# q and k turned on VectorE in blocks, scores on 32-row groups: a change to a fused attention and channel-mix kernel

## The chip, the core and the metric

One NeuronCore of a Trainium2 chip runs the whole program. Five engines work side by side, each through its own fixed sequence of instructions: TensorE (PE; its weight loads are listed apart as PEld), VectorE (DVE), ScalarE (ACT), GpSimd (POOL, here mostly an issuer of DMAs) and SyncE (SP, another issuer). They wait for one another through semaphores. The metric is the device time of one execution in microseconds, as the median of several runs; lower is better.

## What is computed

Sliding-window attention with linear distance biases for 8 batches, 8 heads, 576 positions and 64 dimensions a head, and a channel mix with two gates over its output. Shortened:

```python
scores = scale * q @ k.T                       # per batch and head, 576 x 576
mask = (rel >= 0) & (rel < 128)                # rel = query position - key position
scores = where(mask, scores - slope[h] * abs(rel), -1e9)
attn = softmax(scores);  x = attn @ v          # heads side by side: 576 x 512 a batch
xk = mu_k * x + (1 - mu_k) * x_prev            # x_prev: one position earlier
xr = mu_r * x + (1 - mu_r) * x_prev
out = sigmoid(xr @ w_r) * (relu(xk @ w_k) ** 2 @ w_v)
```

## The kernel before

**Staging.** All matmuls take bf16. A matmul contracts over the partitions, so the scores need q and k with the 64 dimensions of a head on the partitions, while in memory a position's 64 dimensions lie side by side. q and k are therefore loaded with positions on the partitions and turned. Heads go in four pairs, g = 0 to 3, two heads of 64 rows each filling 128 partitions. Positions are cut into four chunks of 128 (SM = 512) and a tail of 64.

**How q and k are turned**, by batch:

- Batch 0 comes first and has its own path in two parts (staging tiles in qx_buf, L1097, L1100 and qk_quad with two runs).
- Batches 1 and 2 (WIDE): wide_load, L463, brings runs of four positions, four heads at a time. qk_quad (L1053) turns each 64x64 block by a matmul against an identity, 32 a head pair; ScalarE or VectorE copies the result from PSUM to qk_buf (L663, a helper that makes every copy).
- Batches 3 to 5: full_load, L498, makes eight loads of 1,024 short runs a batch into cb_buf. qk_some with halves (L804) turns 32 blocks for two head pairs at once; ScalarE copies.
- Batches 6 and 7 (XB): the same loads, but the DMA engines turn them (flip, L502, eight DMA transposes a batch on SP's queue, into qx_buf).
- The tail of 64 positions of each batch is loaded apart into ts_buf (L482, L488), and turned into tt_buf by four matmuls (tails_full, L879; batches 1 to 3) or by one DMA transpose (L595; batches 4 to 7).

**Scores and attention.** For a head pair, `scores` (L693) makes twelve matmuls on 64 rows: six pieces (256, 256, 256, 128, 64, 64 query columns for five key chunks) for each of the two heads, whose row groups 0 to 63 and 64 to 127 work side by side. They fill both two-bank PSUM tiles (duo, class p2). ScalarE makes exp of each half (L707, 128x1024), VectorE multiplies with the exponentials of the bias (L720). `attend` multiplies with v (L749, 18 matmuls), VectorE divides by the row sums (L755, L760) into xu, `out_t` turns xu back (L787; by DMA in batches 6 and 7, L869), and `shift` makes xk and xr (L847, L854 twice).

**Channel mix.** `channel_mix` handles up to 512 positions at once: the matmuls with w_k (L958), relu on ScalarE (L965), the square on VectorE (L931) or ScalarE (L929), the matmuls with w_r (L976) and its tanh (L983), the matmuls with w_v (L992), and the product on VectorE (L997), then the store on SP's queue (L1022). SQ says which engines may square: both in the first three passes, VectorE alone after that.

**Order.** No engine's order is written by hand. Each piece of work becomes a node with engines that may do it, an assumed length, its dependencies, the buffers it takes and frees, and a rank. `Plan.run` plays them through once when the program is built, and emits the instructions in the order found; the chip keeps that order on each engine, so that an instruction which must wait holds all behind it on its engine. `rank` sorts attention by batch and head pair, moved by the tables LEAD and SHIFT per engine, against the channel mix. `paced` holds the turns of a batch back until enough channel mix is planned. `pe_key` lets work on 64 rows follow other work on 64 rows, as TensorE must change its row mode between them. Loads stand in POOL's queue in the order of LOADS, then batch by batch: a (q and k), b (tails), c (v).

Of the kernel before, what the change touches and what calls it, by code (L numbers as in the profile page):

```python
# [9 lines left out]
FP32 = mybir.dt.float32  # L10
# [23 lines left out]
class Plan:  # L34
# [148 lines left out]
def kernel(  # L183
# [30 lines left out]
    NQ, NA, NX, NV, NC = 4, 4, 3, 2, 2  # L214
    XB = range(6, B)
    XO = range(6, B)
    X0 = 16
# [6 lines left out]
    WIDE = (1, 2)  # L224
    PART_WIDE = True
    QK1 = (ACT, DVE)
    TW = (0,)
    QUAD = 0.040
    RUN = {2: 64 * 284 / 345.0, NF: 128 * 284 / 390.0}
# [5 lines left out]
    WAIT = 7.42  # L235
    COST = {'first': 1.28, 'v': 1.15, 'q': 0.944, 'ts': 0.66, 'tv': 0.58, 'w': 0.88, 'run4': 1.0, 'run2': 1.03, 'flip': 1.0, 'mu': 1.0, 'x': 1.0}
    SS = ()
    OH = ()
    QM = 2
    OM = 0  # L240
# [4 lines left out]
    def SQ(order):  # L245
        return (DVE, ACT) if order < 3 else (DVE,)
# [7 lines left out]
    XTT = range(4, B)  # L254
    MMASK = False
    VDEP = 1
    TCOST = 1.5
    KLAST = 1
# [13 lines left out]
    ts_buf = many(2, [128, H, D], BF16, "ts")  # L272
    tt_buf = many(2, [128, G, 3, 64], BF16, "tt")
    qk_buf = many(NQ, [128, 2, SM], BF16, "qk")
    qx_buf = many(2, [128, 2, G, SM], BF16, "qx")
    half_buf = qx_buf[0].rearrange("p i g s -> p (i g s)").rearrange(
        "p (a i r h d) -> p a i r h d", a=2, i=2, r=2, d=D)
    part_buf = qx_buf[0].rearrange("p i g s -> p (i g s)")[:, 2048:4096].rearrange(
        "p (i h r d) -> p i h r d", i=2, r=2, d=D)
    wide_buf = [c.rearrange("p i r h d -> p (i r h d)").rearrange(  # L280
        "p (i h r d) -> p i h r d", i=2, r=NF, d=D) for c in cb_buf]
    stage = qx_buf[1].rearrange("p i g s -> p (i g s)").bitcast(FP32).rearrange(
# [36 lines left out]
    plan = Plan(dict(qx=2, p2=2, p1=N1, pt=4 - N1, qk=NQ, at=NA, xu=NX, vs=NV, cb=NC, ts=2, tt=2, xt=2, dl=2, dl0=4,  # L319
# [10 lines left out]
    def dve_t(n, fast=1):  # L330
# [4 lines left out]
        PE: (19.41, 21.75, 20.3, 20.77, 27.74, 12.48, 14.5, 17.35, 11.67, 21.63),  # L335
        ACT: (-36.25, -14.3, 13.52, -0.46, 8.81, -1.54, 38.45, -38.45, -6.19, 11.9),
        DVE: (-3.5, -13.64, -11.95, 8.63, -28.73, 12.81, 21.66, -2.46, -14.09, 3.03),
# [3 lines left out]
        PE: {(0, 0): 33.45, (1, 0): 0.96, (2, 0): 26.3, (3, 0): 24.3, ('fkk',): -39.43, ('p1', 'fkk'): 4.02, ('p1', 'fxk'): 5.15},  # L341
        ACT: {(1, 0): -17.87, (2, 0): 20.9, (3, 0): 41.7, ('frl',): 48.19, ('rl', 'fp1'): 40.97, ('rs', 'fp1'): -20.02},
        DVE: {(0, 0): -69.5, (1, 0): 89.05, (1, 1): -21.81, (1, 2): -35.86, (2, 0): -19.05, (3, 0): -5.03, ('fp1', 'frs'): -11.82, ('frl',): -102.36, ('ot', 'fp1', 'frs'): 6.45},
# [98 lines left out]

    def blanks(after):
# [8 lines left out]
        for t in range(2):  # L452
            late(tt_buf[t][:, :, 2], 0.0, 0.17)
# [22 lines left out]
    def tail_load(b):  # L476
        h = Hold("ts")
        g = virtual("ts", [h])
        ns = []
        if b in TW:  # L480
            for i in range(2):
                ns.append(dma(POOL, 104, issue_t(128), lambda e, i=i: nc.gpsimd.dma_start(  # L482
                    out=ts_buf[h.idx].rearrange("p h d -> p (h d)")[:, 256 * i:256 * i + 256],
                    in_=(q, k)[i][b, :, SM:S].rearrange("h (c r) d -> h c (r d)", r=4)), [g], kind="ts"))
            return h, ns
        for i in range(2):
            src = (q, k)[i][b, :, SM:S].rearrange("h p d -> p h d")
            ns.append(dma(POOL, 128 * TCOST, issue_t(512), lambda e, i=i, src=src: nc.gpsimd.dma_start(  # L488
                out=ts_buf[h.idx][64 * i:64 * i + 64], in_=src), [g], kind="ts"))
        return h, ns  # L490

    def wide_load(b, h, g, h0, h1):
        return [run_load(lambda: wide_buf[h.idx], i, b, 0, NF, h0, h1, [g]) for i in range(2)]

    def full_load(b, i, h, g):
        src = (q, k)[i][b, :, 0:SM].rearrange(
            "h (r p) d -> p h r d" if b in XB else "h (p r) d -> p h r d", p=128)
        return [dma(POOL, 256, issue_t(1024), lambda e, r=r: nc.gpsimd.dma_start(  # L498
            out=cb_buf[h.idx][:, i, r], in_=src[:, :, r]), [g], kind="q") for r in range(NF)]

    def flip(b, i, j, g):
        return dma(SPE, FLIP * RATE, FISSUE, lambda e: nc.sync.dma_start_transpose(  # L502
            out=qx_buf[xbh[b].idx][:, i, :, 128 * j:128 * j + 128],
            in_=cb_buf[ch[b].idx][:, i, j].rearrange("p h d -> p (h d)")),
            [g, (cl[b][NF * i + j], FWAIT)], (), [ch[b]], FLAT, True)
# [54 lines left out]
    def load_step(what):  # L560
# [14 lines left out]
        elif what == "t":  # L575
            th[0], tl[0] = tail_load(0)
# [12 lines left out]
    cw, ch, cl, xbh, xbl, tth, ttl, ttg = {}, {}, {}, {}, {}, {}, {}, {}  # L589

    def tail_flip(b):
        htt, hs = Hold("tt"), th[b]
        g = plan.add(VIR, 0.0001, 0.0001, [], (0,), None, [htt])
        tth[b], ttg[b] = htt, g
        ttl[b] = [dma(SPE, FLIP * RATE, FISSUE, lambda e: nc.sync.dma_start_transpose(  # L595
            out=tt_buf[htt.idx][:, :, 0:2].rearrange("p g t c -> p g (t c)"),
            in_=ts_buf[hs.idx].rearrange("p h d -> p (h d)")),
            [g] + [(x, FWAIT) for x in tl[b]], (), [hs], FLAT, True)]

    def batch_load(b, what):  # L600
        if what == "a":
            ch[b] = Hold("cb")
            g_ = virtual("cb", [ch[b]])
            if b not in WIDE:
                cl[b] = full_load(b, 0, ch[b], g_) + full_load(b, 1, ch[b], g_)
            else:
                cw[b] = [wide_load(b, ch[b], g_, 4 * j, 4 * j + 4) for j in range(2)]
        elif what == "b":
            th[b], tl[b] = tail_load(b)
            if b in XB:  # L610
                xbh[b] = Hold("qx")
                g_ = virtual("qx", [xbh[b]])
                xbl[b] = [flip(b, i, j, g_) for i in range(2) for j in range(NF)]
            if b in XTT:
                tail_flip(b)
# [49 lines left out]
    def scores(b, g, parts, bias, hq, ha, deps, prio, need, free):  # L665
# [9 lines left out]
        def emit(e):  # L675
            qk = qk_buf[hq.idx] if hq.cls == "qk" else qx_buf[hq.idx][:, :, g]
# [119 lines left out]
    def halves(n, block):  # L796

        hp = [Hold("p1"), Hold("p1")]

        def emit(e):  # L800
            for i in range(n):
                src, c = block(i)
                for r in range(2):
                    nc.tensor.transpose(  # L804
                        one(hp[r]).bitcast(BF16)[:, c:c + 64], src[64 * r:64 * r + 64],
                        ident[64 * r:64 * r + 64, 64 * r:64 * r + 64])

        return hp, emit
# [492 lines left out]
```

## Time and profile before

| What | Value |
|---|---|
| median of three runs (lowest, highest) | 235.77 us (235.13, 236.39) |
| span of the profiled execution | 233.9 us |
| granted TensorE clock in it | full (1.000) |
| DMA, share of the POOL-issued queue's packets in 16 engines' span | 97.6%, 96,016 packets |
| loads of q and k into cb, issue to landing (median) | 6.8 to 7.5 us for 128 KB, 10.0 to 10.3 us for 256 KB |
| turns by DMA into qx (16) | 7.8 us each, issue to landing |

The span runs from the first to the last instruction of one execution. The profile names an instruction by its source line and the tiles that it writes and reads, without buffer numbers. Busy time of TensorE is a union of overlapping matmuls, whose single lengths (some 190 ns for a small one) include the array's latency; what a block costs the engine is read from the chain of waits or from the distance between starts. Durations on DVE and ACT stand as they are. ScalarE's copies to qk take 616 ns on average (37 of 128x512), its exp of 128x1024 takes 1,039 ns (56 of them), VectorE's mask product 684 ns (56), its quotient xu 819 ns (28).

### The profile page before, as it was taken

The page shows a single profiled execution, that of the slowest core. Times are in us where ns is not written, and L with a number is a line of the kernel's source. Part 1 is how long each engine was busy: PE and PEld are TensorE (multiplying, and loading weights), DVE is VectorE, ACT ScalarE, POOL GpSimd, SP SyncE. Part 2 cuts the span into 40 slices and gives each one's busy share as a digit, 9 for nine tenths or more (in the row PEclk, how much of TensorE's full clock was granted, in tenths as well). Part 3 has the DMA queues.
Part 4 walks back from the last instruction along what each step waited for, and adds up shares of the span by engine and source line. Part 5 has one row for each costly group of instructions (what it writes and reads, how often), then busy time and mean ns, then how long its engine had stood idle before and what let it go on. Part 6 is the DMA issues. An engine that isn't in the chain of part 4 may idle for free.

```text
span 233.9 us, 6461 instructions
## 1 busy us (share of the span) xinstructions
PE 225.3 (96%) x2586; PEld 138.3 (59%) x2615; DVE 189.6 (81%) x424; ACT 164.7 (70%) x294; POOL 93.5 (40%) x120
## 2 busy tenths in 40 slices
PE   8999799999999999999999999979999999999994
PEld 7676666665756755555855765535564744445462
DVE  7497998999998999887999999879899965324252
ACT  3769998979986969979997585845674626236261
POOL 8796655679972980794195740000000000000000
PEclk9999999999999999999999999999999999999999
DMA  7999999999999999899999999952314121121212
GB/s 172 184 163 193 187 170 201 193 172 192 157 143 126 145 143 179 70 163 175 127 189 108 180 158 206 169 93 92 118 32 121 69 76 45 46 90 48 90 45 90
DMA packets 121565, 31.09 MB, mean 133 GB/s; under 512 B 108216, under 2 KB 117696, under 8 KB 121536
## 3 DMA queue, kind: packets, MB, share of 16 engines
q0 software_dynamic: 96016, 16.26, 97.6%
q1 hardware_dynamic: 23776, 13.84, 27.0%
q10 hardware_dynamic: 1744, 0.59, 1.1%
q8 instruction: 20, 0.33, 0.6%
q14 instruction: 9, 0.07, 0.1%
HBM read 33.56 MB, written 9.44 MB: 184 GB/s over the span
## 4 chain that ended last, share of the span: by engine, by line
PE 75%; DMA 13%; DVE 4%; ACT 3%; issue 2%; POOL 1%; POOLq 0%; DVEq 0%; ACTq 0%
PE uno L992 25%; PE uno L958 21%; PE uno L976 12%; PE duo L749 6%; PE duo L693 5%; DMA ts<-in_k_dram 4%; DMA xt<-xu 3%; DMA wk_sb<-in_moe_w_k_dram 3%; DMA vs<-in_v_dram 3%; PE uno L787 3%; ACT at L707 2%; PE uno L1053 1%; PE uno L804 1%; DVE kk L931 1%; POOL vs L467 1%
## 5 line engine op out<-in xcount | busy, mean ns | idle before, releaser
L992 PE MATMUL uno<-wv_sb,kk 128*128 128x512 bf16 (+2 forms) x277 | 70.8, 373 | 1.5 <-DVE kk L931 0.5
L707 ACT ACTIVATE at<-duo 128x1024 bf16<-128x1024 f32 (+2 forms) x68 | 63.9, 986 | 8.5 <-PE duo L693 8.5
L958 PE MATMUL uno<-xk,wk_sb 128*128 128x256 bf16 (+2 forms) x412 | 69.1, 313 | 0.6
L965 ACT ACTIVATE rl<-uno 128x256 bf16<-128x256 f32 (+2 forms) x104 | 46.8, 481 | 13.3 <-PE uno L958 11.5
L958 PEld LDWEIGHTS <-wk_sb 128*128 128x128 bf16 x416 | 38.5, 98 | 20.2 <-issue 0.2
L983 ACT ACTIVATE rs<-uno 128x512 bf16<-128x512 f32 x36 | 21.7, 606 | 34.5 <-PE uno L976 32.5
L992 PEld LDWEIGHTS <-kk 128*128 128x128 bf16 x296 | 26.8, 98 | 28.3 <-DVE kk L931 1.3
L997 DVE SCALAR_TENSOR_TENSOR ot<-rs,uno 128x512 f32<-128x512 bf16 (+2 forms) x37 | 24.8, 669 | 19.7 <-PE uno L992 16.3
L467 POOL DMA_DIRECT2D vs<-in_v_dram x32 | 28.4, 903 | 28.7 <-PE duo L749 21.3
L720 DVE TENSOR_TENSOR at<-at,mask 128x1024 bf16<-128x1024 bf16 x56 | 37.3, 684 | 2.2 <-ACT at L707 2.0
L976 PE MATMUL uno<-wr_sb,xr 128*128 128x512 bf16 x138 | 36.7, 379 | 0.9 <-DVE ot L997 0.5
L931 DVE TENSOR_TENSOR kk<-rl 128x256 bf16<-128x256 bf16 (+2 forms) x96 | 31.3, 340 | 7.6 <-ACT rl L965 6.2
L854 DVE SCALAR_TENSOR_TENSOR xr<-dl,mu_sb,xt 128x576 bf16<-128x576 bf16 (+1 forms) x32 | 24.9, 779 | 0.3
L854 DVE SCALAR_TENSOR_TENSOR xk<-dl,mu_sb,xt 128x576 bf16<-128x576 bf16 (+1 forms) x32 | 24.6, 778 | 0.0
L749 PEld LDWEIGHTS <-at 128*128 128x128 bf16 x576 | 21.5, 98 | 5.1 <-issue 0.6
L663 ACT COPY qk<-uno 128x512 bf16<-128x512 bf16 (+1 forms) x40 | 21.3, 598 | 3.4 <-PE uno L1053 1.7
L760 DVE TENSOR_TENSOR xu<-duo,rc 128x640 bf16<-128x640 f32 x28 | 22.7, 819 | 0.2
L976 PEld LDWEIGHTS <-xr 128*128 128x128 bf16 x144 | 13.5, 98 | 15.9 <-issue 0.7
L498 POOL DMA_DIRECT2D cb<-in_k_dram x20 | 17.7, 922 | 5.0 <-DMA vs<-in_v_dram 3.2
L749 PE MATMUL duo<-vs,at 128*128 128x65 bf16 x448 | 19.1, 194 | 0.1
L498 POOL DMA_DIRECT2D cb<-in_q_dram x20 | 17.8, 924 | 1.7 <-DMA cb<-in_k_dram 0.7
L663 ACT COPY xt<-uno 128x576 bf16<-128x576 bf16 (+2 forms) x28 | 15.9, 578 | 2.4 <-PE uno L787 2.3
(81 smaller groups left out, 209.1 us busy)
## 6 DMA issues: line engine op xcount, KB each, us to landing
out_dram<-ot SPq DMA_DIRECT2D x30, 256.0 KB, 5.5
vs<-in_v_dram POOLq DMA_DIRECT2D x32, 128.0 KB, 7.6
cb<-in_q_dram POOLq DMA_DIRECT2D x20, 128.0 KB, 6.8
cb<-in_k_dram POOLq DMA_DIRECT2D x20, 128.0 KB, 7.5
out_dram<-ot SPq DMA_DIRECT2D x10, 128.0 KB, 1.7
wk_sb<-in_moe_w_k_dram POOLq DMA_DIRECT2D x2, 512.0 KB, 7.6
cb<-in_q_dram POOLq DMA_DIRECT2D x4, 256.0 KB, 10.0
cb<-in_k_dram POOLq DMA_DIRECT2D x4, 256.0 KB, 10.3
```

The costliest lines, as they stand in the source:

```text
L467: return dma(POOL, 256, issue_t(1024), lambda e: nc.gpsimd.dma_start(out=vs_buf[h.idx][:, j, :, 0:D], in_=v[b, :, 128 * j:128 * j + 128].r ...
L498: return [dma(POOL, 256, issue_t(1024), lambda e, r=r: nc.gpsimd.dma_start(out=cb_buf[h.idx][:, i, r], in_=src[:, :, r]), [g], kind="q") f ...
L663: (nc.scalar.copy if e == ACT else nc.vector.tensor_copy)(out=out, in_=in_)
L707: lambda e, ah=ah, w=w, hp=hp: nc.scalar.activation(out=ah(), in_=two(hp)[:, :, 0:w], func=AF.Exp, scale=float(scale)), (), [hp])
L720: nc.vector.tensor_tensor(out=a, in0=a, in1=m, op=ALU.mult)
L749: nc.tensor.matmul(a[:, hl, t - t0], lhsT=at[:, lo:lo + 128], rhs=vs[:, u, 2 * g + hl, :] if u < NF else tvb[:, 2 * g + hl], start=(u == u ...
L854: lambda e: nc.vector.scalar_tensor_tensor(out=buf[hk.idx][:, g, e0 + c0:e0 + c1], in0=dls(), scalar=mu[:, g:g + 1], in1=xc(1), op0=ALU.mu ...
L931: nc.vector.tensor_tensor(out=out, in0=in_, in1=in_, op=ALU.mult)
L958: nc.tensor.matmul(one(hp)[:, 0:n], lhsT=wk_sb[:, po, 128 * fo:128 * fo + 128], rhs=xk_buf[hx.idx][:, po, c0:c1], start=(po == 0), stop=(p ...
L965: a = op(ACT, act_t(n), [s], pr, lambda e, hp=hp, hr=hr: nc.scalar.activation(out=rl_buf[hr.idx][:, 0:n], in_=one(hp)[:, 0:n], func=AF.Rel ...
L976: nc.tensor.matmul(one(hp), lhsT=xr_buf[hx.idx][:, po, 128 * c:128 * c + 128], rhs=wr_sb[:, po], start=(po == 0), stop=(po == NPO - 1))
L992: nc.tensor.matmul(one(hv)[:, a:b], lhsT=kk_buf[hk.idx][:, fo, o:o + 128], rhs=wv_sb[:, fo, a:b], start=(fo == 0), stop=(fo == NFO - 1))
```

## The change

In batches 1 to 7 there is one path for q and k. `quad_load` loads four heads over 128 partitions: partition 32h + p holds 18 consecutive positions of head h, 4,608 adjacent bytes in memory, 1,152 bf16 in SBUF, the tail of 64 positions included. There are four such loads a batch (q and k, two quartets). `turn` reads such a row as 576 words of four bytes, that is two neighbouring dimensions, and transposes its eighteen 32x32 blocks in one VectorE instruction. Afterwards partition 32h + w holds the dimensions 2w and 2w+1 of every position, position by position, in qt_buf: dimensions of even and of odd number lie at every second bf16. `scores4` then makes the scores of four heads at once on the row groups 0, 32, 64 and 96: two accumulating matmuls a piece, one over the even and one over the odd dimensions, in two halves that each fill both duo tiles. Key chunk 4 has 64 positions; the other 64 columns are set to zero once (n_pad).

What falls away: wide_load, full_load, flip, tails_full, tail_flip, qk_some and qk_full, the copies to qk and the separate tail loads of batches 1 to 7. The first three steps of batch 0 keep their path; their bf16 copies now lie in the second raw buffer. Squares of every pass may run on either engine. The planner's tables (LEAD, SHIFT, COST, WAIT) have other numbers, and pe_key groups 32-row work too.

```diff
-        if rows == 64 and n.rows[0] == 64:
+        if rows != 128 and n.rows[0] == rows:
             return (-1e8,) + tuple(key)
...
     def SQ(order):
-        return (DVE, ACT) if order < 3 else (DVE,)
+        return (DVE, ACT)
...
-    cb_buf = many(NC, [128, 2, NF, H, D], BF16, "cb")
+    raw_buf = many(NC, [128, 2, 2, TB * D], BF16, "raw")
+    qt_buf = many(NT, [128, S + KW, 2], BF16, "qt")
...
+    def quad_load(b, i, c, h, g):
+        src = (q, k)[i][b, 4 * c:4 * c + 4].rearrange("h (p r) d -> (h p) (r d)", r=TB)
+        return dma(POOL, QUADKB, issue_t(128), lambda e: nc.gpsimd.dma_start(
+            out=raw_buf[h.idx][:, i, c], in_=src), [g], kind="quad")
...
-            if b not in WIDE:
-                cl[b] = full_load(b, 0, ch[b], g_) + full_load(b, 1, ch[b], g_)
-            else:
-                cw[b] = [wide_load(b, ch[b], g_, 4 * j, 4 * j + 4) for j in range(2)]
-        elif what == "b":
-            th[b], tl[b] = tail_load(b)
...
+            cl[b] = [[quad_load(b, i, c, ch[b], g_) for i in range(2)] for c in range(2)]
...
+    def turn(b, c):
+
+        hq, n, res = Hold("qt"), None, []
+        for i in (1, 0):
+            def emit(e, i=i):
+                nc.vector.transpose(
+                    out=qt_buf[hq.idx][:, S * i:S * i + S].rearrange("p s t -> p (s t)").bitcast(FP32)
+                    .rearrange("p (q t) -> p t q", t=TB),
+                    in_=raw_buf[ch[b].idx][:, i, c].bitcast(FP32).rearrange(
+                        "p (t w) -> p t w", w=32))
...
+    def scores4(b, c, half, hq, has, deps):
+
+        pieces, m0 = (QUAD0, QUAD1)[half]
...
+            for (u, q0, n) in pieces:
+                c0 = BASE[u] + q0 - 128 * u - a0
+                for t in range(2):
+                    for j in range(4):
+                        r = 32 * j
+                        nc.tensor.matmul(
+                            two(hps[j // 2])[:, j % 2, c0:c0 + n],
+                            lhsT=qt[r:r + 32, S + 128 * u:S + 128 * u + 128, t],
+                            rhs=qt[r:r + 32, q0:q0 + n, t],
+                            start=(t == 0), stop=(t == 1), skip_group_check=True)
...
+        for c in range(2):
+            hq, y = turn(b, c)
+            has = [Hold("at"), Hold("at")]
+            s0, m0 = scores4(b, c, 0, hq, has, y)
+            s1, m1 = scores4(b, c, 1, hq, has, y + [(s0, 0.0)])
+            for j in range(2):
+                g = 2 * c + j
+                prio = (0, b, 0, g)
+                r, hx = attend(b, g, 0, NJ, has[j], [m0[j], m1[j]] + vl[b], prio)
```

The pieces are QUAD0 = (chunk 0, 256 columns; chunk 1, 256) and QUAD1 = (chunk 2, 256; chunk 3, 192; chunk 4, 64). There are two raw buffers (NC = 2, a batch each) and three qt buffers (NT = 3, a quartet each).

More of the change, by code (lines that the diff above doesn't have):

```diff
@@ L223 @@
     RATE = 284.0
[L224 to L227, printed above, removed]
     QUAD = 0.040
-    RUN = {2: 64 * 284 / 345.0, NF: 128 * 284 / 390.0}
+    RUN = {2: 64 * 284 / 345.0}
+    QUADKB = 576 * 284 / 390.0
     FLIP = 1.0
@@ L451, in blanks @@
             late(tv_buf[t][0:64, :, D], 1.0)
-        for t in range(2):
-            late(tt_buf[t][:, :, 2], 0.0, 0.17)
+        late(tt_buf[0][:, :, 2], 0.0, 0.17)
+        n_pad.extend(dve_op(0.1, lambda e, t=t: nc.vector.memset(qt_buf[t][:, 2 * S:S + KW], 0.0),
+                            [after], (0, 31)) for t in range(NT))
         for t in range(NA):
@@ L587, in load_step @@
             batch_load(1, what)
[L589 to L598, printed above, removed]
+    ch, cl = {}, {}
     def batch_load(b, what):
@@ L894, in tails @@
         hs = th[b]
-        if b in XTT:
-            plan.follow(last["tt"], ttg[b])
-            last["tt"] = ttg[b]
-            return tth[b], ttl[b]
-        if b not in TW:
-            return tails_full(b, prio, htt, hs)
         hp = Hold("p1")
@@ L922 @@
     of = out.rearrange("b s m -> (b s) m")
-    n_hw = 39 + sum(4 if g in FT else 2 for g in range(3)) + 8 * len(XB) + len(XTT) + G * len(XO)
+    n_hw = 39 + sum(4 if g in FT else 2 for g in range(3)) + G * len(XO)
     n_split = -n_hw % 8
@@ L1060, in qk_quad @@
         w = 64 * nr
-        ys = [op(QK0 if b == 0 else QK1, {ACT: act_t(2 * w), DVE: dve_t(2 * w)}, [t], prio + (3,),
+        ys = [op(QK0, {ACT: act_t(2 * w), DVE: dve_t(2 * w)}, [t], prio + (3,),
                  lambda e, r=r: copy_any(
```

256 lines of the change are left out of this document (66 added, 190 removed).

## The prediction

> **What bounds the kernel now.** I read the busy shares first, then the chain of waits, then the stages.
>
> ```profile
> span 233.9 us, 6461 instructions
> PE 225.3 (96%) x2586; PEld 138.3 (59%) x2615; DVE 189.6 (81%) x424; ACT 164.7 (70%) x294; POOL 93.5 (40%) x120
> ...
> PE   8999799999999999999999999979999999999994
> ...
> DVE  7497998999998999887999999879899965324252
> ACT  3769998979986969979997585845674626236261
> ```
>
> TensorE is busy nearly everywhere, VectorE is full for two thirds of the span and half idle after that. A busy TensorE is not proof, so the chain of waits decides: 75% of it is TensorE, and its largest other share, 13% DMA, lies mostly in the first 28 us. From about 30 us on, TensorE's own instructions follow one another, and what it executes is what the span costs:
>
> ```profile
> 42.38 0.49 PE uno L1053 x32
> ...
> 43.42 0.55 PE duo L693 x12
> 43.97 0.38 PE uno L1053 x32
> ...
> 60.80 0.57 PE uno L804 x32
> ...
> 62.12 0.22 PE uno L879 x4
> ...
> 65.09 0.56 PE uno L787 x10
> 65.64 0.55 PE duo L693 x12
> ```
>
> Columns: start, length, line, count. L1053, L804 and L879 are the turns of q and k by identity matmuls; L693 is one head pair's scores. All stand on the path. The stages (busy us of each engine in a stretch):
>
> ```profile
> 24.00:36.00 12.00, 10.70 (x238) 8.07 (x237) 11.35 (x28) 11.77 (x28) 7.14 (x10) 1.00 1.86 180
> 36.00:140.00 104.00, 102.74 (x1366) 65.31 (x1383) 98.39 (x197) 89.43 (x157) 68.20 (x82) 1.00 1.90 156
> 140.00:200.00 60.00, 58.29 (x463) 31.66 (x471) 50.78 (x103) 34.90 (x56) 0.00 (x0) 1.00 0.55 100
> 200.00:234.00 34.00, 30.70 (x171) 16.58 (x172) 11.55 (x26) 12.38 (x25) 0.00 (x0) 1.00 0.20 70
> ```
>
> The order is PE, PEld, DVE, ACT, POOL. The change takes work from TensorE, where it pays at once, and puts some on VectorE, which from 36 to 140 us has 5.6 us free of 104. That is the question of this case.
>
> **The sum.** Terms are against the profiled execution, 233.9 us; the median of the runs, 235.77 us, lies 1.9 us above it.
>
> *Turns taken off TensorE.* Batches 3 to 5: 192 matmuls of L804 in 6 blocks of 0.57 us, 3.4 us. Batches 1 and 2: 256 of L1053 in 8 blocks of 0.38 to 0.52 us, 3.4 us. Tails: three blocks of L879 at 0.22 us, 0.7 us. Batches 6 and 7 have none: their q and k are turned by DMA. **-7.5 us.**
>
> *Scores on 32-row groups.* Today a pair of heads costs 0.55 us, so four heads cost 1.10 us. The chain's eight L992 matmuls of 512 columns in 1.73 us give 0.42 ns a column. A pair streams 256+256+256+128+64+64 = 1024 columns in each of two row groups at once: 0.43 us, so 0.12 us of each block is fill and switching. New: 256+256+256+192+64 columns, twice because each matmul holds half of the 64 dimensions: 2048 columns, 0.86 us for four heads if all four groups stream at once, plus two fills of 0.12, 1.10 us: no change, **0**. No row shows four groups, nor operands read at every second element. Lower end: fills hidden, 14 x -0.24 = -3.4 us. Upper end: groups go two at a time or the step of two halves the stream, 14 x 0.86 = +12 us. I take 0, since two groups start 4 ns apart in the present score blocks and 32 loads and 32 matmuls of L804 pass in 0.57 us (18 ns a pair), so that four pairs (72 ns) fit under 256 columns (108 ns).
> The Trainium skill, in "TensorE: Matmul & The Clock Gate", section "Measured speedup vs the span model", gives four row groups 3.07 times one at 512 columns, not 4. By that as an estimate 0.86 becomes 1.12 us, and the sum would end 14 x 0.26 = 3.6 us higher. No run here shows it yet.
>
> *Turns put on VectorE.* 28 instructions (7 batches, two quartets, q and k) of 576 four-byte words a partition. The nearest row is one element a cycle over the same count:
>
> ```profile
> L854 DVE SCALAR_TENSOR_TENSOR xr<-dl,mu_sb,xt 128x576 bf16<-128x576 bf16 x28 | 22.7, 812 | 0.3
> L447 DVE MEMSET at<- 128x64 bf16 x4 | 0.3, 112 | 0.0
> L429 DVE MEMSET vs<- 128x32 bf16 x2 | 0.2, 85 | 0.1
> ```
>
> 0.81 us each, 22.7 us in all. They write words 72 bytes apart. The vs memset writes 32 elements 130 bytes apart in 85 ns, the at memset 64 adjacent ones in 112 ns: fewer elements, proportionally less time, no visible price for the distance. Bounds: 0.41 us (two a cycle) and 1.41 us (two cycles a word). I take 0.81.
> The Trainium skill's "SBUF — State Buffer", section "Specifications (TRN2)", says that a 16-byte line needs two hits for full bandwidth and that crossing to a new line costs; each of these writes crosses. The memset row speaks against it, and the second rival below is what it would do.
>
> *What else VectorE and ScalarE give and take.* Off VectorE: 5 copies to qk of 0.69 us and 3 to tt of 0.42 us, -4.7 us. Off ScalarE: about 35 copies to qk at 0.62 us, -21.6 us. In the dense stretch VectorE gets about 20 turns, +16.2, less 2.1 for its copies: 112.5 us of work for 104, unless squares leave. Squares of all passes may now go to ScalarE; the stretch has 43 of them, 13.3 us, on VectorE. ScalarE there has 89.4 - 16.3 (copies to qk) = 73.1 us, and 43 squares at some 0.5 us (L929 takes 0.45 at 256 columns, 0.56 at 384) make it 94.6. So both fit, VectorE at 99.2, hardly any slack, in a stretch that TensorE would leave after some 98. What doesn't fit slides behind 140 us, where VectorE has 9.2 free of 60 and then 22 of 34, and the channel mix still owed there keeps TensorE busy meanwhile. What this costs: a score block queued behind a late turn holds every later TensorE instruction, since each engine's order is fixed. I take **+1 us**, from 0 to +10.
>
> *DMA.* Off the POOL queue: 40 loads at 0.92 us, 8 at 0.75 and 14 tail loads at 0.71 (q, k) against 28 new ones at about 0.65 (the 128-descriptor tail loads of L482, 0.61 to 0.68): 53 us of issuing becomes 18. The same bytes come in 4.6 KB runs. The first scores of batch 1 no longer wait for the tail load, which ends at 27.5 us on the chain, nor for a copy to qk (0.40 and 0.72 us of idle TensorE), but for a turn on a full VectorE: between 0 and -1.1, **-0.5**. Off the SP queue: 16 DMA turns to qx and 4 to tt, 1.2 us of issue each. The eight of xt that stay had one late by 7.7 us at 145.8, and TensorE idles 1.45 us from 140 to 160; between 0 and -1.5, **-0.5**. The v loads keep their place and wait for the same attend blocks as before (21.3 us of POOL waits). Batch 2 now lands in the buffer that held batch 0's bf16 copies, which were read by 17 us, while its loads start at 30.7: nothing. Three pad memsets at 0.11 us, and the smaller memsets dropped: nothing.
>
> Sum: -7.5 + 0 + 1 - 0.5 - 0.5 = -7.5, so 226.4 us in the profile and **228.3 us** as measured.
>
> **Rivals.**
> *VectorE takes over.* If the turns come in front of what the masks and quotients need, or squares stay on VectorE, the dense stretch costs TensorE part of what it gained. For it: 112.5 us of work against 104. Against: attention is ahead, the last score block is at 179.6 us with 54 us of channel mix behind it. With about half the gain returned, 232.5 us.
> *The turn costs two cycles a word.* 28 x 0.60 = 16.8 us more; 24 turns of that before 140 us, 14.4 us, less the 6.3 us that VectorE has free from 24 to 140, puts 8.1 us on TensorE's waits: 236.4 us, no gain. For it: the 72-byte step, nowhere seen with four-byte words. Against: the vs memset.
> *Slower: the scores do not run four abreast.* One place, L693's successor: 14 quartets at 1.96 instead of 1.10 us, +12.1 us, 240.4 us. It decides from 7.5 / 14 = 0.54 us a quartet on. For it: no instruction here uses 32-row groups, strided weights or two accumulating passes. Against: the 4 ns between two groups.
> *The block turn is not one instruction* but one for each 32x32 block: it would act as the second rival, only worse; nothing in the profile speaks for it, and it is counted there.
>
> **How the numbers follow.** Forecast 0.58 (its own range 225 to 231.5); VectorE takes over 0.16; slow turn 0.10; slow scores 0.16. The range 223.5 to 239 begins at 228.3 - 3.4 (both fills hidden) - 1.4 (most of the 1.6 between the values taken for DMA and their lower ends) and leaves out the slow scores. What can be told from no change is 0.5%, 234.6 to 237.0 us: faster has nearly all of the forecast, most of the second case and a little of the third, 0.73; same 0.07; slower 0.20.
>
> **What would show it.** No identity matmuls on qk, TensorE about 7.5 us less busy; four heads' scores at 1.1 us, in two blocks of 0.55, with the four groups' starts a few ns apart; turns at 0.8 us; ScalarE's squares up from 8 to some fifty; VectorE below its present total plus 5 us. I am wrong if score blocks last 0.8 us or more, if turns take 1.2 us or more, or if TensorE idles more than 5 us behind turns.

## The result and the profile after

The change made the kernel slower. The time after is 238.15 us, the median of 4 runs (237.35 to 239.1); the kernel before took 235.45 us on the same chip (4 runs, 234.89 to 236.39). The ratio is 1.0124, with a 95% interval of 1.0079 to 1.0169. The forecast was 228.3 us, so 9.9 us are to be found.

The page of the kernel after (its profile is of the slowest of the four runs), from its busy shares, its granted clock, its DMA queues and its chain of waits (shares of the span, first by engine, then by line):

```profile
span 237.3 us, 5923 instructions
PE 223.6 (94%) x2379; PEld 131.1 (55%) x2379; DVE 198.8 (84%) x401; ACT 165.6 (70%) x304; POOL 58.1 (24%) x86
...
PEclk9999979999999999999799999999999999999999
...
q0 software_dynamic: 46832, 16.26, 62.9%
...
PE 50%; DVE 30%; DMA 12%; issue 4%; ACT 2%; POOL 0%; DVEq 0%; POOLq 0%
...
L1061 DVE STREAM_TRANSPOSE qt<-raw 128x576 f32<-128x576 f32 x28 | 34.5, 1248 | 0.0
```

TensorE's share of the chain fell from 75% to 50%, and VectorE now has 30% of it. The turns (L1061) take 1.248 us each, where 0.81 was forecast. The granted clock drops in two slices. GpSimd's issuing fell as forecast (93.5 to 58.1 us of busy time), and its queue carries the same bytes in half as many packets.

The stages of the kernel after. The columns are the length, then the busy us of PE, PEld, DVE, ACT and POOL, then the granted clock, the DMA share and GB/s:

```profile
24.00:36.00 12.00, 10.29 (x121) 5.95 (x120) 11.86 (x24) 11.04 (x23) 5.12 (x9) 0.86 1.77 181
36.00:140.00 104.00, 99.02 (x1123) 58.96 (x1120) 99.16 (x174) 81.96 (x148) 31.22 (x45) 0.98 0.98 136
140.00:200.00 60.00, 58.80 (x613) 32.31 (x612) 57.63 (x103) 44.05 (x76) 4.21 (x5) 1.00 0.42 81
200.00:240.00 40.00, 33.78 (x188) 17.94 (x186) 13.36 (x30) 12.97 (x26) 0.00 (x0) 0.97 0.19 73
```

In the dense stretch from 36 to 140 us TensorE idles 5.0 us where it idled 1.3 us before, and part of its busy time is at a lower clock. VectorE has gone from 50.8 to 57.6 us of 60 in the stretch behind it. Work was pushed back: after 200 us TensorE still owes 33.8 us, against 30.7.

Where does TensorE stop? Its waits, in us, times and longest:

```profile
PE uno L860 <- DVE ot L899: 4.1, 3, 2.2
PE duo L1084 <- ACT at L1101: 2.1, 3, 1.0
PE duo L1084 <- DVE qt L1061: 1.4, 3, 1.0
```

The longest is a new one. L860, the first matmul of the channel mix, waits for the output product L899 to free a PSUM bank. And L899 itself waits. The chain of waits around the two places (start, length, line):

```profile
49.07 0.53 DVE ot L899
49.62 6.03 DMA out_dram<-ot
55.75 0.69 DVE ot L899
...
106.16 7.42 DMA out_dram<-ot
113.68 0.70 DVE ot L899
114.42 3.63 PE uno L860 x12
```

A store issued at 49.62 us lands 6.03 us later, and only then may a product write the same output buffer. The same happens at 106.16 us. The timeline shows which products lie between (the bracket is the idle time before the instruction and what ended it; only products and the matmuls that wait for them are shown):

```profile
48.91 0.68 DVE L899 SCALAR_TENSOR_TENSOR ot<-rs,uno 128x512 f32<-128x512 bf16 x1
51.32 0.68 DVE L899 SCALAR_TENSOR_TENSOR ot<-rs,uno 128x512 f32<-128x512 bf16 x1
53.02 0.68 DVE L899 SCALAR_TENSOR_TENSOR ot<-rs,uno 128x512 f32<-128x512 bf16 x1
55.75 0.69 DVE L899 SCALAR_TENSOR_TENSOR ot<-rs,uno 128x512 f32<-128x512 bf16 x1 [1.32 <-DMA out_dram<-ot]
56.49 1.78 PE L860 MATMUL uno<-xk,wk_sb 128*128 128x384 bf16 x10 [1.69 <-DVE ot L899]
...
105.44 0.69 DVE L899 SCALAR_TENSOR_TENSOR ot<-rs,uno 128x512 f32<-128x512 bf16 x1
107.95 0.71 DVE L899 SCALAR_TENSOR_TENSOR ot<-rs,uno 128x512 f32<-128x512 bf16 x1
113.68 0.69 DVE L899 SCALAR_TENSOR_TENSOR ot<-rs,uno 128x512 f32<-128x512 bf16 x1 [1.98 <-DMA out_dram<-ot]
114.42 3.63 PE L860 MATMUL uno<-xk,wk_sb 128*128 128x384 bf16 x12 [2.20 <-DVE ot L899]
```

The product at 55.75 us is the third after the one whose store it waits for, and that at 113.68 us the second after. There are five output buffers, but the planner that writes the order hands out the lowest-numbered one that it believes free, and its model gives a buffer back 3.9 us after the product where no other transfer is in the way (0.6 to issue, 1.0 and 0.8 in transit, 1.5 to land). Note also the last row: twelve matmuls of 384 columns take 3.63 us. Right behind the gap TensorE's granted clock is halved, from 114.13 to 117.54 us; it was halved once before, from 32.21 to 35.62 us. The other runs had less of this: the mean clocks of the four are 0.985, 0.993, 0.993 and 1.000, from the slowest (239.1 us) to the fastest (237.35 us). So the clock explains only some 0.8 us of the median.

### The profile page after: what moved, and what is told of

The parts are those of the page before. It is cut to its first block, busy times and chain, and to the rows that moved or that the text cites. A ratio compares the mean times of both kernels' runs of the same rounds, so it can differ in the third digit from the quotient of the medians.

```text
span 237.3 us, 5923 instructions
## 1 busy us (share of the span) xinstructions
PE 223.6 (94%) x2379; PEld 131.1 (55%) x2379; DVE 198.8 (84%) x401; ACT 165.6 (70%) x304; POOL 58.1 (24%) x86
## 4 chain that ended last, share of the span: by engine, by line
PE 50%; DVE 30%; DMA 12%; issue 4%; ACT 2%; POOL 0%; DVEq 0%; POOLq 0%
PE uno L860 15%; PE uno L894 15%; DVE qt L1061 9%; PE uno L878 9%; DMA out_dram<-ot 6%; DVE at L1111 5%; PE duo L709 4%; DVE xu L720 4%; DMA ts<-in_k_dram 3%; PE duo L1084 3%; DVE ot L899 3%; DMA vs<-in_v_dram 3%; DVE xr L780 3%; DVE xk L780 3%; DVE dl L773 2%
## 5 line engine op out<-in xcount | busy, mean ns | idle before, releaser
L860 PE MATMUL uno<-xk,wk_sb 128*128 128x256 bf16 (+2 forms) x416 | 74.1, 319 | 4.1 <-DVE ot L899 4.1
L1101 ACT ACTIVATE at<-duo 128x1024 bf16<-128x1024 f32 x56 | 54.8, 1035 | 7.0 <-PE duo L1084 6.9
L860 PEld LDWEIGHTS <-wk_sb 128*128 128x128 bf16 x416 | 39.0, 99 | 30.7 <-issue 9.4
L899 DVE SCALAR_TENSOR_TENSOR ot<-rs,uno 128x512 f32<-128x512 bf16 (+2 forms) x37 | 24.6, 669 | 16.0 <-PE uno L894 12.6
L1111 DVE TENSOR_TENSOR at<-at,mask 128x1024 bf16<-128x1024 bf16 x56 | 36.6, 680 | 0.3 <-ACT at L1101 0.3
L878 PE MATMUL uno<-wr_sb,xr 128*128 128x512 bf16 x144 | 36.1, 386 | 0.0
L1061 DVE STREAM_TRANSPOSE qt<-raw 128x576 f32<-128x576 f32 x28 | 34.5, 1248 | 0.0
L885 ACT ACTIVATE rs<-uno 128x512 bf16<-128x512 f32 x36 | 21.2, 612 | 18.7 <-PE uno L878 12.3
L833 DVE TENSOR_TENSOR kk<-rl 128x256 bf16<-128x256 bf16 (+2 forms) x53 | 17.8, 339 | 10.9 <-ACT rl L867 10.1
L831 ACT ACTIVATE kk<-rl 128x256 bf16<-128x256 bf16 (+2 forms) x51 | 25.2, 517 | 0.6
L709 PEld LDWEIGHTS <-at 128*128 128x128 bf16 x576 | 20.9, 98 | 4.7 <-DVE at L1111 0.5
L1084 PE MATMUL duo<-qt 32*128 32x256 bf16 (+2 forms) x560 | 18.7, 254 | 3.6 <-ACT at L1101 2.1
L1084 PEld LDWEIGHTS <-qt 32*128 32x128 bf16 x560 | 12.2, 93 | 14.0 <-issue 9.5
```

Of the source, the lines that this page charges most:

```text
L709: nc.tensor.matmul(a[:, hl, t - t0], lhsT=at[:, lo:lo + 128], rhs=vs[:, u, 2 * g + hl, :] if u < NF else tvb[:, 2 * g + hl], start=(u == u ...
L860: nc.tensor.matmul(one(hp)[:, 0:n], lhsT=wk_sb[:, po, 128 * fo:128 * fo + 128], rhs=xk_buf[hx.idx][:, po, c0:c1], start=(po == 0), stop=(p ...
L878: nc.tensor.matmul(one(hp), lhsT=xr_buf[hx.idx][:, po, 128 * c:128 * c + 128], rhs=wr_sb[:, po], start=(po == 0), stop=(po == NPO - 1))
L899: nc.vector.scalar_tensor_tensor(out=ot_buf[ho.idx][:, a:b], in0=rs_buf[hs.idx][:, a:b], scalar=1.0, in1=one(hv)[:, a:b], op0=ALU.add, op1 ...
L1061: nc.vector.transpose(out=qt_buf[hq.idx][:, S * i:S * i + S].rearrange("p s t -> p (s t)").bitcast(FP32) .rearrange("p (q t) -> p t q", t=TB),
L1084: nc.tensor.matmul(two(hps[j // 2])[:, j % 2, c0:c0 + n], lhsT=qt[r:r + 32, S + 128 * u:S + 128 * u + 128, t], rhs=qt[r:r + 32, q0:q0 + n, t],
```

## The experiments

The first eight experiments test two theories on top of each other: that the slow turn costs what is missing, and that the waits for stores do. The last four take the second apart. Ratios are against the kernel before on the same chip; one per cent is 2.35 us. In kernels with added lines, line numbers move by a few.

### 1. The write made dense

```diff
-                    .rearrange("p (q t) -> p t q", t=TB),
+                    .rearrange("p (t q) -> p t q", t=TB),
```

> The changed kernel with one edit: the turn writes its eighteen 32x32 blocks one after the other (adjacent words) instead of interleaved, 72 bytes from word to word. Positions then stand in another order in qt, so the scores are not the reference's; the same instructions in the same order, the same sizes. Theory A (the write step makes the turn slow, 1.25 us against the 0.81 us that I counted): turns at about 0.8 us, 28 x 0.45 = 12.6 us off VectorE, and most of it comes back because VectorE is on the chain: 228 to 232 us, faster than the kernel before. Rival B (a four-byte turn costs 1.25 us however it writes): turns still 1.25 us, 238 us. Rival C (VectorE's order and load are the trouble, not the length of a turn): turns at 0.8 us but still 235 us or more.

Measured: 233.83 us, ratio 0.9954 (0.9921 to 0.9987). The turn is as theory A had it, the time 1.8 us above its range.

```profile
L1061 DVE STREAM_TRANSPOSE qt<-raw 128x576 f32<-128x576 f32 x28 | 21.2, 761 | 0.0
```

The same instruction over the same words takes 0.761 us when its 32 words of a row lie side by side, so the 72-byte write step costs 0.49 us a turn. Against the ratio of 1.0124, the kernel gains 1.7%, 4.0 us. The waits of the product for a store stay, 3.8 us in two places.

### 2. The step by size

Positions are loaded in runs of r, so that the write step is 4r bytes: r = 18, 9, 6, 3, 2, 1 and 18 in batches 1 to 7. Batches with shorter runs are loaded by one transfer a head.

```diff
-        src = (q, k)[i][b, 4 * c:4 * c + 4].rearrange("h (p r) d -> (h p) (r d)", r=TB)
+            src = (q, k)[i][b, 4 * c + j].rearrange("(j p r) d -> p j (r d)", p=32, r=r)
...
-                    .rearrange("p (q t) -> p t q", t=TB),
+                    .rearrange(*(("p (q t) -> p t q",) if RL[b] == TB else ("p (j q r) -> p j r q",)),
+                               **(dict(t=TB) if RL[b] == TB else dict(r=RL[b], q=32))),
```

> Batches 1 to 7 load runs of 18, 9, 6, 3, 2, 1 and 18 positions for each partition (shorter runs by one DMA a head), so that the turn writes words 72, 36, 24, 12, 8, 4 and 72 bytes apart; the result stays the reference's. A look at the length of the turn only. Theory A: 1.25 us at 72 bytes, the same or little less at 36 and 24, and a fall to 0.8 us where several words share 16 bytes, that is at 8 and 4 bytes, 12 in between. Rival B: 1.25 us in all batches.

Measured: 232.69 us in a single run. One turn of batches 1 to 6 each, from the timeline:

```profile
30.57 1.24 DVE L1070 STREAM_TRANSPOSE qt<-raw 128x576 f32<-128x576 f32 x1
...
60.64 1.21 DVE L1070 STREAM_TRANSPOSE qt<-raw 128x576 f32<-128x576 f32 x1
...
78.47 1.22 DVE L1070 STREAM_TRANSPOSE qt<-raw 128x576 f32<-128x576 f32 x1
...
90.07 0.96 DVE L1070 STREAM_TRANSPOSE qt<-raw 128x576 f32<-128x576 f32 x1
...
116.10 0.77 DVE L1070 STREAM_TRANSPOSE qt<-raw 128x576 f32<-128x576 f32 x1
...
130.34 0.77 DVE L1070 STREAM_TRANSPOSE qt<-raw 128x576 f32<-128x576 f32 x1
```

Steps of 72, 36 and 24 bytes cost the same, 12 bytes a part of it, 8 and 4 bytes nothing. That fits a line of 16 bytes: from 24 bytes on every word stands alone in its line, at 8 bytes two words share one. At 12 bytes two of every four words stand alone, which would be half the price, 0.77 + 0.5 x 0.47 = 1.0 us; 0.96 was measured. The Trainium skill, "SBUF — State Buffer", section "Specifications (TRN2)", names lines of 16 bytes, two hits a line for full bandwidth, and a penalty for each crossing. The trace agrees on the two hits, not on a penalty for each crossing: at 8 bytes every second word opens a new line and costs nothing. It adds the size: (1.24 - 0.77) / 576 = 0.8 ns a word that stands alone.

### 3. The order written with the turn's true price

The planner reckoned 0.1 us above the adjacent rate for a turn.

```diff
-    TURN = 0.1
+    TURN = 0.58
```

> The changed kernel with one number of the planner: a turn counted with 1.25 us instead of 0.77 us, so that the orders of all engines are drawn up for the length it has. Rival D (the loss is an order drawn up for a shorter turn, so that instructions queue behind late turns): 231 to 234 us, and idle TensorE between 36 and 200 us goes from about 8 us to 3 us. Theory A (the work itself is too much for VectorE in the dense stretch, whatever the order): 236 to 239 us, the waits only move.

Measured: 244.62 us, ratio 1.0393 (1.0322 to 1.0463), worse than the change itself and outside both forecasts. TensorE's longest waits:

```profile
PE uno L860 <- DVE xk L780: 4.8, 2, 4.2
PE duo L1084 <- ACT at L1101: 2.7, 4, 1.1
```

One constant gives another order, with a gap of 4.2 us at another place. The tables of due times were fitted with the old constant, so this run doesn't test the price; it shows that the order alone can cost several us.

### 4. Runs of two positions in all batches

The edit of experiment 2 with r = 2 in batches 1 to 7: 112 loads of one head instead of 28 of four.

> All batches 1 to 7 with runs of two positions (512 bytes in memory), so words are written 8 bytes apart; the result stays the reference's. 112 loads of a head each instead of 28 of four heads. Theory A: turns at 0.8 us, the attention stage no longer late, 229 to 233 us if the loads, four times as many to issue (112 x 0.63 = 71 us of POOL, where the kernel before spent 53 us), keep up; if they do not, waits for raw appear and it ends at 234 to 238 us. Rival B: turns at 1.25 us and 238 us or more.

Measured: 234.83 us, ratio 0.998 (0.9944 to 1.0016), the second case of the expectation. The turns take 0.766 us and no product waits for a store. But with 84 more loads to issue, GpSimd brings batch 1 and a weight late:

```profile
24.00:36.00 12.00, 6.76 (x80) 4.04 (x79) 9.27 (x21) 8.14 (x18) 11.32 (x17) 0.85 1.52 138
```

TensorE does 6.76 us of work in these 12 us against 10.29 in the kernel after. The gain elsewhere is spent here.

### 5. Nine output buffers

Four more buffers in the staging tile, which is idle after the start, and all nine taken in turn. The order of the instructions is unchanged.

```diff
+    def ot_of(ho):
+        if not hasattr(ho, "at"):
+            ho.at = len(given) % (NO + 4)
+            given.append(ho)
+        return ot_buf[ho.at] if ho.at < NO else more[:, 512 * (ho.at - NO):512 * (ho.at - NO) + 512]
...
-                    out=ot_buf[ho.idx][:, a:b], in0=rs_buf[hs.idx][:, a:b], scalar=1.0,
+                    out=ot_of(ho)[:, a:b], in0=rs_buf[hs.idx][:, a:b], scalar=1.0,
```

> The changed kernel with nine output buffers in turn instead of five (four of them in the staging tile qx, idle after 17 us); the order of all instructions stays. Theory S (the loads of a whole batch, now issued in a burst, keep stores waiting 6 to 7 us, a product on VectorE waits for its output buffer, and TensorE stands behind it: 1.85 us at 54 and 2.36 us at 112 us of the changed kernel, with the granted clock down behind such gaps): both gaps go, 233 to 236 us. Rival: the gaps only move to the next late thing on a full VectorE: 237 us or more.

Measured: 233.89 us, ratio 0.9945 (0.9911 to 0.998). Both waits are gone, with the turns still at 1.237 us: 1.8%, 4.2 us. So the slow turn isn't the whole loss, and the waits aren't either.

### 6. Both: dense write and nine buffers

The edits of experiments 1 and 5.

> Adjacent words from the turn (positions in another order, so the scores are not the reference's) and nine output buffers. If both theories hold and add: the 233.8 us of the dense write alone less the 2.05 and 1.88 us that TensorE idles at 54 and 110 us there: 229 to 231 us. If they overlap: 232 to 234 us.

Measured: 229.18 us, ratio 0.9732 (0.9666 to 0.9799). Against the change that is 3.9%, 9.2 us. The parts measured alone, 4.0 and 4.2, add up to 8.2: within the intervals they add. With both losses out, 229.2 us is 0.9 us from the forecast of 228.3.

### 7. Nearly no turn, five buffers

```diff
-        n_pad.extend(dve_op(0.1, lambda e, t=t: nc.vector.memset(qt_buf[t][:, 2 * S:S + KW], 0.0),
+        n_pad.extend(dve_op(0.1, lambda e, t=t: nc.vector.memset(qt_buf[t], 0.0),
...
-                    out=qt_buf[hq.idx][:, S * i:S * i + S].rearrange("p s t -> p (s t)").bitcast(FP32)
-                    .rearrange("p (q t) -> p t q", t=TB),
-                    in_=raw_buf[ch[b].idx][:, i, c].bitcast(FP32).rearrange(
-                        "p (t w) -> p t w", w=32))
+                    out=qt_buf[hq.idx][:, S * i:S * i + S].rearrange("p s t -> p (s t)").bitcast(FP32)[:, 0:32],
+                    in_=raw_buf[ch[b].idx][:, i, c].bitcast(FP32)[:, 0:32])
```

> Each turn reduced to one of its eighteen blocks (the rest of qt stays zero, so the scores are not the reference's), some 0.1 us each; loads, scores and all orders as in the changed kernel. What the change would be with the turns nearly free. If VectorE's turns are the whole loss: 226 to 229 us, the saving on TensorE that I counted. If the start of batch 1 and the stores keep their part: 231 to 233 us, little under the dense write's 233.8.

Measured: 235.56 us, ratio 1.001 (0.9973 to 1.0048), above both forecasts, with these rows for the turn, for the clearing of the qt buffers, and for the waits of the product and of TensorE:

```profile
L1061 DVE STREAM_TRANSPOSE qt<-raw 128x32 f32<-128x32 f32 x28 | 5.3, 195 | 0.0
...
L448 DVE MEMSET qt<- 128x1216 uint32 x3 | 3.2, 1072 | 0.6 <-issue 0.4 <-PE uno L999 0.2
```

```profile
DVE ot L899 <- DMA out_dram<-ot: 3.8, 2, 2.3
...
PE duo L653 <- DVE qk L623: 1.1, 1, 1.1
```

29 us of turns are gone and the kernel is still no faster than before the change. VectorE's load isn't the whole answer either: the waits for stores stay, and with them the lower clock (0.83 from 108 to 118 us). A part is the experiment's own price: it clears the three qt buffers whole at the start, 1.07 us each where the padding took 0.11, and TensorE waits 1.1 us for the copy to qk behind them.

### 8. A whole kernel: runs of two, nine buffers

Batch 1 keeps its runs of 18, since its loads are the urgent ones (experiment 4); batches 2 to 7 have runs of 2 and with them the 8-byte step; nine output buffers.

```diff
+    RL = {b: 18 if b == 1 else 2 for b in range(1, 8)}
```

> Batches 2 to 7 in runs of two positions (words 8 bytes apart), batch 1 in runs of 18 as in the change, so that its four loads are not late, and nine output buffers; the result stays the reference's. If turn, start and stores are the three parts of the loss: 229 to 232 us, faster than the kernel before. If the many small loads or the first batch's slow turns still hold TensorE: 233 to 235 us.

Measured: 229.63 us, ratio 0.9769 (0.9714 to 0.9824). The turns are whole here and the positions stand in their order, and the kernel is faster than both.

```profile
PE 218.0 (96%) x2347; PEld 130.7 (57%) x2379; DVE 191.2 (84%) x401; ACT 164.3 (72%) x304; POOL 102.9 (45%) x158
...
PEclk9999999999999999999999999999999999999999
```

TensorE's busy time is 7.3 us below the 225.3 of the kernel before, near the 7.5 us of the forecast's first term. It shows here since no matmul runs at a lower clock; in experiments 1 and 5, whose traces have the full clock too, it is 6.1 us below.

### 9. Five buffers, taken in turn

No buffer added; experiment 5's function with `ho.at = len(given) % NO`.

> The changed kernel with its five output buffers taken in turn; before, each product took the lowest-numbered buffer that the written order believed to be free, so the product at 55.75 us stood behind the store issued at 49.62 us, only three products earlier. No buffer is added. Theory (the choice of buffer, with stores that take 6 to 7 us, makes the wait): both waits for a store go, and the time comes to the 233.9 us of nine buffers, 233.5 to 235. Rival (five buffers are too few for stores so late): a wait of over 1 us for a store stays in at least one of the two places, 236.5 to 238.5 us. A third possibility, that the waits were paid back by something else all along, would leave 238 without any wait for a store.

Measured: 233.57 us, ratio 0.9926 (0.9886 to 0.9967), the same as with nine. No wait for a store is left, and the second place now looks like this:

```profile
107.14 0.68 DVE L906 SCALAR_TENSOR_TENSOR ot<-rs,uno 128x512 f32<-128x512 bf16 x1
...
110.79 0.68 DVE L906 SCALAR_TENSOR_TENSOR ot<-rs,uno 128x512 f32<-128x512 bf16 x1
111.52 2.11 PE L867 MATMUL uno<-xk,wk_sb 128*128 128x384 bf16 x12
```

The twelve matmuls take 2.11 us, not 3.63, and nothing stands ahead of them. The stores are as late as they were (median landing 6.7 us from 48 to 56 us, up to 7.3 from 100 to 118). So five buffers are enough; the loss was in which one was taken. Until this run I had put it down to too few buffers.

### 10. Control: the kernel before, five buffers in turn

The same edit in the kernel before.

> Control: the kernel before with its own five output buffers taken in turn. Its trace has 1.2 us of waits of the product for a store in two places, 0.8 us the longest. Theory (the wait for stores is a loss that the change brought): at most 1 us faster than the kernel before, 234.3 to 235.5. Rival (the kernel before pays for its buffers too, and the change has no part in it): 231 to 233.5.

Measured: 234.29 us, ratio 0.9964 (0.993 to 0.9997): 0.8 us. The kernel before has the same way of choosing, and its stores were late too (5.3 to 6.3 us from 40 to 60 and from 98 to 116 us), yet it lost little: from 40 to 60 us its products stand at 41.56, 42.76, 50.00 and 54.45, while the kernel after has four between 48.91 and 55.75. The loss came with the change, by the new order.

### 11. The loads cut by head

Each load of 288 KB becomes four of 72 KB with the same runs of 4.6 KB.

```diff
-        return dma(POOL, QUADKB, issue_t(128), lambda e: nc.gpsimd.dma_start(
-            out=raw_buf[h.idx][:, i, c], in_=src), [g], kind="quad")
+        return [dma(POOL, QUADKB / 4, issue_t(32), lambda e, j=j: nc.gpsimd.dma_start(
+            out=raw_buf[h.idx][32 * j:32 * j + 32, i, c], in_=src[32 * j:32 * j + 32]), [g], kind="quad")
+            for j in range(4)]
```

> The changed kernel with each load of 288 KB for four heads cut into four loads of 72 KB, one head each, over 32 partitions; the runs of 18 positions, the order on all engines and the five buffers as chosen by the written order stay, and GpSimd issues 84 loads more. Theory A (the size of a transfer in the queue delays the stores): the stores of the two places land in 3 to 4 us and the waits go, 234 to 235.5. Theory B (the bytes asked for in one burst delay them, however they are cut): the waits of 1.3 and 2.0 us stay, 237 to 239. Either way the turns stay at 1.25 us.

Measured: 237.92 us, ratio 1.0087 (1.0037 to 1.0136). Neither theory got both halves. Theory A was right on the waits: none is left, and the stores land in 4.5 to 6.0 us at the first place and 3.3 to 4.9 at the second, where they took 5.7 to 7.2 and up to 7.4. But the time is that of theory B, for another reason, seen in TensorE's longest wait and in the stage that holds it:

```profile
PE uno L879 <- DMA wr_sb<-in_moe_w_r_dram: 3.0, 1, 3.0
```

```profile
24.00:36.00 12.00, 7.12 (x88) 4.36 (x87) 11.15 (x22) 8.78 (x19) 9.06 (x14) 0.86 1.49 140
```

As in experiment 4, the 84 additional loads make a weight late on the same queue, and 3.2 us of TensorE's work slip out of this stage. Cutting all loads is the wrong cure. What delays the stores isn't settled by this run: the loads are smaller, but they are also asked for more slowly (at the second place four loads of 1.15 MB in all are issued within 2.2 us in the kernel after, and sixteen within 11 us here), so size and pace changed together.

### 12. Nearly no turn, nine buffers

The edits of experiments 5 and 7.

> The changed kernel with nine output buffers and with each turn cut to one of its 18 blocks (scores computed from zeros but for one block). If what is left of the loss beyond the slow write is the turns' own work on VectorE, this ends below the 229.2 us of the dense write with nine buffers, by up to 28 x 0.57 = 16 us at the very most; theory: VectorE has room, so by 0 to 2 us, 227 to 229.5. Rival (VectorE is the bound once the stores are out of the way): below 226.

Measured: 231.13 us, ratio 0.9808 (0.9751 to 0.9865), no faster than the 0.9732 (0.9666 to 0.9799) of the whole turn at 0.76 us. Once a turn takes 0.76 us, what is left of it costs nothing that these runs can tell. The expected 227 to 229.5 us was missed on the upper side. A part of the 1.9 us to experiment 6 is again the clearing of the qt buffers, for which TensorE waits at the start:

```profile
PE duo L653 <- DVE qk L623: 1.8, 1, 1.8
```

Experiment 6 has no such wait, and the scores of batch 1 behind the wait of 0.95 us start at 29.72 us there and at 31.39 us here. How much of this is the clearing isn't settled: in the profiled executions without it they start anywhere from 29.72 to 31.31 us (experiment 1), and the intervals of the two ratios meet.

## Why the prediction was wrong, step by step

**Turns taken off TensorE, -7.5 us: right.** Hidden in part in the kernel after, where slowed matmuls fill the time (-1.7 us of busy time), and shown at full clock by experiment 8 (-7.3 us).

**Scores on 32-row groups, 0: right.** The chain of the kernel after has the blocks, one for half the keys of four heads:

```profile
66.03 0.57 PE duo L1084 x24
...
144.00 0.57 PE duo L1084 x14
151.60 0.57 PE duo L1084 x23
154.87 0.56 PE duo L1084 x16
```

Two of 0.57 us a quartet, against 1.10 forecast; 28 x 0.02 us more is 0.6. The four groups of a piece start within 10 ns of one another (65.963 to 65.973 us in the first of these blocks). Nothing in the total points to a price for operands read at every second element. The slowdown that the prediction worked out at +3.6 us from the Trainium skill's figure for four row groups isn't seen at this size, and the rival of slow scores (0.16) falls.

**Turns put on VectorE, 0.81 us each: the step that failed.** The prediction argued from the memset row that a wide step has "no visible price for the distance". A turn costs 1.248 us instead, 12.3 us more in all, and experiments 1 and 2 show that all the excess over 0.76 is the step. (Its two bounds weren't made alike either: 0.41 us halves the whole 0.81, 1.41 adds 0.60 to it.) The sum of the second rival, with the measured excess over 0.81 in place of its 0.60 us, gives 24 x 0.44 - 6.3 = 4.3 us. Experiment 1 takes 0.49 us off a turn, for which the same sum gives 5.5; it measured 4.0, and from experiment 5 to 6, where no product waits for a store, 5.0 (0.9945 - 0.9732). So that rival was the right mechanism with a smaller size, and it had a chance of 0.10: I let a memset of 32 elements, another instruction, speak louder than a rule on the memory that each of these writes breaks.

**VectorE's lateness, +1: right at the price that it assumed.** With the turn at 0.76 us and the stores out of the way the sum comes to 229.2 us (experiment 6), and taking nearly all of the turns away brings no more (experiment 12). VectorE is full in the dense stretch, as the prediction had it; that 99.16 us were measured where 99.2 were forecast is luck, since each turn took 0.44 us more than was counted and other work slid behind 140 us. TensorE's waits behind the turns themselves are only 1.4 us, well under the 5 us that the prediction named as a sign.

**DMA, -0.5 and -0.5, and a term that was missing: the sum's other failed step.** The second half came: TensorE idles 0.2 us from 140 to 160 us, where it idled 1.45. Batch 1 gained nothing: its first scores stand 0.68 and 0.95 us behind the exponentials that free their PSUM banks, 1.63 us of idle TensorE where it was 1.12. The two together are some 0.3 us off. What was missing altogether was the output side. The prediction listed what the loads do to GpSimd's queue and never asked which product reuses which output buffer, and how long after the store. It took the products' places for fixed, though the change has the whole order written anew. Stores that land late were there before (5.3 to 6.3 us); products close enough to meet them were not. That cost 4.7 us by experiment 9 (1.0124 - 0.9926) and 4.2 by experiment 5, in some executions part of it through the clock behind the gaps.

4.0 for the step and 4.7 for the buffers are 8.7 of the 9.9 us, and both together measured 9.2. The remaining 0.7 us is within the intervals. "VectorE takes over" (0.16) would have ended at 232.5 us and had the place right, VectorE from 36 to 140 us; its cause, masks and squares in front, wasn't what happened: ScalarE took 51 squares of 104.

One of the signs named in the prediction decided at first sight: turns at 1.2 us or more. It says only that the sum is off by one term, not that this is all; had I stopped there, half of the loss would have been put to the wrong account.

Not tried: runs of two with the five buffers taken in turn, which by experiments 8 and 9 should do without the staging tile; and an order fitted anew to the true price of the turn.

## What to carry to other kernels

A strided write is priced by the line that it touches and by the instruction that makes it: look for a row of the same engine that writes at the same step with the same kind of operation, and where there is none, let the rule set the end of the range rather than a short memset. When a change has an order written anew, check who reuses each buffer and how long after its last transfer; the number of buffers says little if the lowest one is always taken. And take losses out one at a time and together: two of about 4 us that add look, from either side alone, like a theory that failed.

## What the runs showed of the hardware

The price of a write step on VectorE's block turn of 128x576 four-byte words was 1.24 us at 72 bytes, 1.21 at 36, 1.22 at 24, 0.96 at 12 and 0.77 at 8 and 4. From the 195 ns of 32 words and the 761 ns of 576, an adjacent word costs (761 - 195) / 544 = 1.04 ns. The memset of 32 two-byte elements at 130 bytes, 85 ns, lies on the line of the adjacent ones (112 ns for 64 elements and, in experiment 7, 1,072 for 1,216) and shows no such price; why a memset escapes it stays open.

The granted clock is not told by the length of one gap. It was halved after gaps of 0.68 and 0.95 us, and again after one of 2.20 us, but not after one of 1.69 us, nor in experiment 1 after one of 1.89 us. In the traces it is halved for 3.41 us or twice that, and the full-clock stretches between are multiples of 3.41 us too (78.51 is 23 times it). Laid on that grid, the kernel after has these rows (length, busy us of PE, PEld, DVE, ACT and POOL, granted clock, DMA share, GB/s):

```profile
28.80:32.21 3.41, 1.78 (x30) 1.09 (x29) 3.41 (x7) 3.41 (x7) 1.08 (x2) 1.00 2.54 152
32.21:35.62 3.41, 3.38 (x24) 1.12 (x22) 3.41 (x8) 2.81 (x5) 1.32 (x3) 0.50 1.48 189
52.69:56.10 3.41, 2.11 (x28) 1.01 (x21) 2.09 (x5) 2.85 (x4) 1.09 (x2) 1.00 1.82 216
110.72:114.13 3.41, 1.50 (x36) 1.23 (x35) 1.43 (x3) 3.38 (x7) 0.00 (x0) 1.00 1.02 249
114.13:117.54 3.41, 3.12 (x10) 1.43 (x10) 3.41 (x7) 1.23 (x3) 0.00 (x0) 0.50 0.28 96
```

A stretch in which TensorE was busy for 1.78 or 1.50 of the 3.41 us is followed by a halved clock, one with 2.11 us isn't. Over the traces of all runs, the end of each left out, there are twelve such stretches at full clock with TensorE busy for less than 1.9 us: eleven were followed by a halved clock (the exception is in experiment 1), and none with more was. Where the grid lies against the gaps differs from execution to execution. The Trainium skill, "TensorE: Matmul & The Clock Gate", section "HAM oscillation — how this bites in real kernels", puts the gap that matters at about 3.4 us; here shorter ones were enough. Twelve matmuls then took 3.63 us instead of 2.11, so the wait of 2.2 us cost 3.7 in this execution.
